# Four gate and up chunks by single token tiles, tile 1's LN2 transposed by DMA, W_down loaded later in halves

## The chip, the cores and the metric

The kernel runs on one core of a Trainium2 chip. The metric is the device time of one launch in microseconds (us), given as the median of the shown runs. The kernel before takes 271.42 us (three runs: 271.40, 271.42 and 271.55).

## The reference

One transformer block over 2048 tokens of width 640 in bf16: a layer norm, a linear attention of 32 heads of 20 with learned feature maps, the residual, a second layer norm and a gated feed-forward net of width 1536.

```python
def _A_ref(x, wqkv, w_phi, wo):
    qkv = (x @ wqkv).reshape(B, S, 3, H, Dh).transpose(2, 0, 3, 1, 4)
    q, k, v = qkv[0], qkv[1], qkv[2]
    pq = jnp.einsum("bhsd,hdf->bhsf", q, w_phi)
    pk = jnp.einsum("bhsd,hdf->bhsf", k, w_phi)
    phi_q = jnp.concatenate([_softmax(pq), _softmax(-pq)], axis=-1)
    phi_k = jnp.concatenate([_softmax(pk), _softmax(-pk)], axis=-1)
    kv = jnp.einsum("bhsf,bhsd->bhfd", phi_k, v)
    z = jnp.einsum("bhsf->bhf", phi_k)
    num = jnp.einsum("bhqf,bhfd->bhqd", phi_q, kv)
    den = jnp.einsum("bhqf,bhf->bhq", phi_q, z)[..., None] + 1e-6
    return (num / den).transpose(0, 2, 1, 3).reshape(B, S, D) @ wo

def _B_ref(x, w_gate, w_up, w_down):
    return (_gelu(x @ w_gate) * (x @ w_up)) @ w_down

h = x + _A_ref(_layernorm(x), A_wqkv, A_w_phi, A_wo)
h2 = h + _B_ref(_layernorm(h), B_w_gate, B_w_up, B_w_down)
```

## The kernel before

The 2048 tokens are 16 tiles of 128, in four blocks of four tiles. The kernel has two phases. The first normalises x (LN1), forms V and the key features of every tile and sums the attention state KV over all tiles. The second, which the change touches, forms the query features (q_mm, q_exp), applies the state to each token tile, projects with Wo, adds the residual, normalises again (LN2) and runs the gated net.

**The steps of a token tile t in the second phase.** attn_a: 40 small matmuls (tile "ab", L586) apply the state; their results are copied from PSUM to SBUF as AB (L653), by ScalarE or, with the argument dve, by VectorE. attn_b and attn_b2: denominators and weights, pr, den and w on GpSimd and the reciprocal rd on VectorE. attn_b3: on VectorE tt (L683) and o (L687), then a DMA on SyncE's queue transposes o into oT. attn_c: the projection with Wo, 10 matmuls into po (L708). attn_d: VectorE adds the residual into x_sb and takes a sum. attn_d2: ScalarE squares, GpSimd works out mean and deviation. attn_e: ScalarE writes the normalised ln (L151), and it is transposed into LN2T, a block's 512 columns wide. Tiles 0 and 1 are treated apart, ahead of the others: their ln comes from VectorE (L156), tile 0's goes through a DMA transpose (L167), tile 1's, by attn_e(1, True, True) at L879, through five TensorE transposes into a PSUM tile "tp" (L164) that VectorE copies out (L165).

**The gated net.** gate_up(b, f, a0, a1) at L759 is one chunk: 128 of the 1536 hidden columns for the tokens a0 to a1 of block b. Five matmuls with W_gate and five with W_up (L768), the token columns moving, give the two halves of a PSUM tile gu; ScalarE writes the gelu g (L771), VectorE the product GT (L774). For block 0 the first round takes 256 tokens (tiles 0 and 1), 12 chunks, the next round the other 256; later blocks take 512. down(b, tl, u, ...) at L776 multiplies one token tile's 12 chunks of GT with W_down (L790), each chunk's GT as the loaded weight, in the order f = 0 to 11, and VectorE adds the residual (L792).

**What sets the order.** Every engine's order is that of the program, which is written out by hand. weave(units, stages) at L811 goes through a list of units (the chunks, then the W_down products); ahead of unit i it runs the stages whose number is at most i. attn_at(t, i, offs) at L885 gives the unit numbers of tile t's eight steps as i plus an offset; a negative offset leaves a step out, as tile 2's attn_a is called ahead of the weave (L882).

**PSUM.** Until the stage split, at unit 12, all of these results share a pool of four tiles, two banks each (gtile, L111, bufs=4 at L80): pq, tp, each of the two tiles of an ab, po, and each gu. A tile is taken again once its last reader is done. After split the banks are handed out singly.

**DMA.** All the DMAs of this phase are issued on SyncE's queue, in program order; an issue that waits holds up those behind it. load_down((f, n)) loads n of the 12 parts of W_down: nine parts at L870, three as a stage at unit 6 (L898).

Of the kernel before, what the change touches and what calls it, by code (L numbers as in the profile page):

```python
# [8 lines left out]
BF16 = mybir.dt.bfloat16  # L9
F32 = mybir.dt.float32  # L10
ALU = mybir.AluOpType
ACTF = mybir.ActivationFunctionType
# [5 lines left out]
def kernel(  # L18
# [12 lines left out]
    nc = tc.nc  # L31
    P = 128
# [7 lines left out]
    NC = D // P  # L40
    NF = FF // P
# [46 lines left out]
    Wg = const.tile([P, NC, FF], BF16, name="Wg")  # L88
    Wu = const.tile([P, NC, FF], BF16, name="Wu")
# [6 lines left out]
    Eq = [const.tile([P, len(g), 2, 512], BF16, name=f"Eq{j}") for j, g in enumerate(QG)]  # L96
# [14 lines left out]
    def gtile(name):  # L111
        return psG.tile([P, 2, 512], F32, name=name, tag="G")
# [46 lines left out]
    def transpose_to(dst, src, on_pe, on_dve=False):  # L159

        if on_pe:
            tp = psG.tile([P, 16, P], BF16, name="tp", tag="G")
            for c in range(NC):
                nc.tensor.transpose(tp[:, c, :], src[:, c * P:(c + 1) * P], ident)  # L164
            (nc.vector.tensor_copy if on_dve else nc.scalar.copy)(dst, tp[:, 0:NC, :])  # L165
        else:
            nc.sync.dma_start_transpose(dst, src)  # L167
# [219 lines left out]
    def q_mm(j, part=(0, 1), kcs=range(NC)):  # L387

        if 0 in part and 0 in kcs:
            pqs[j] = gtile("pq")  # L390
        for i, bc in enumerate(QG[j]):
            if i not in part:
                continue
            b, c = divmod(bc, NC)
            for kc in kcs:
                nc.tensor.matmul(pqs[j][:, i, :], lhsT=Wq2[:, kc, c * P:(c + 1) * P], rhs=LN1T[b][:, kc, :],  # L396
                                 start=(kc == 0), stop=(kc == NC - 1))

    def q_exp(j, signs=(0, 1)):
        for s in signs:  # L400
            nc.scalar.activation(Eq[j][:, :, s, :], pqs[j][:, 0:len(QG[j])], ACTF.Exp, scale=(1.0, -1.0)[s])  # L401
# [135 lines left out]
    q = len(QT)  # L537
# [10 lines left out]
    p2 = ctx.enter_context(tc.tile_pool(name="p2", bufs=1, reuse_waits="tile"))  # L548
    p2r = ctx.enter_context(tc.tile_pool(name="p2r", bufs=1, side="right", reuse_waits="tile"))
    Wd = p2r.tile([P, NF, D], BF16, name="Wd")  # L550
# [6 lines left out]
    def load_down(*fs):  # L557

        for f, n in fs:
            nc.sync.dma_start(Wd[:, f:f + n], wd_v[:, f:f + n])  # L560
# [3 lines left out]
    LN2T, st = {}, {}  # L564
# [6 lines left out]
    def bank(name):  # L571
        return psB[0].tile([P, 512], F32, name=name, tag="B")

    def attn_a_mm(t):

        b = t // 4
        if b not in LN2T:
            LN2T[b] = p2.tile([P, NC, 512], BF16, name="LN2T", bufs=2)
        st[t, "ab"] = gtile("ab"), gtile("ab")
        ab = [x[:, i] for x in st[t, "ab"] for i in range(2)]  # L580
        for s in range(2):
            for c in range(NC):
                i, h, n = SLOT[c]
                h += s * QH
                for r, q in enumerate(QUAD):
                    nc.tensor.matmul(ab[r][:, h * KC:(h + n) * KC], lhsT=eq(t, c, s)[q],  # L586
                                     rhs=KV[s][q, i:i + n, 1 - s:1 - s + KC],
                                     start=(s == c == 0), stop=(s == 1 and c == NC - 1), skip_group_check=True)
        st[t] = ab
# [59 lines left out]
    def attn_a(t, dve=0):  # L649
        attn_a_mm(t)  # L650
        AB, ab = ABs[t % 2], st[t, "ab"]
        for u in ((1, 0) if t in (4,) else (0, 1)):
            (nc.vector.tensor_copy if u >= 2 - dve else nc.scalar.copy)(  # L653
                AB[:, :, u * UH:(u + 1) * UH].rearrange("p s (r h) f -> p r s (h f)", r=2),
                ab[u][:, :, 0:2 * QH * KC].rearrange("p r (s x) -> p r s x", s=2))
        st[t] = AB
# [73 lines left out]
    def attn_ds(t, between=None):  # L730

        st[t] = ln_stats(p2, [x_sb[t // 4][:, t % 4, :]], "2", False, between)[0]
# [17 lines left out]
    def attn_ln(t, on_pe=False):  # L750
        st[t] = (ln_dve if on_pe else ln_act)(p2, "2", *st[t])

    def attn_e(t, on_pe=False, on_dve=False):
        if on_pe is False:
            attn_ln(t)
        ln = st[t]
        transpose_to(LN2T[t // 4][:, :, t % 4 * P:(t % 4 + 1) * P], ln, on_pe, on_dve)

    def gate_up(b, f, a0, a1):  # L759
        if psB:  # L760
            gu = bank("gu"), bank("gu")
        else:
            gu = gtile("gu")
            gu = gu[:, 0], gu[:, 1]
        n = a1 - a0
        for i, W in ((0, Wg), (1, Wu)):
            for c in range(NC):
                nc.tensor.matmul(gu[i][:, 0:n], lhsT=W[:, c, f * P:(f + 1) * P], rhs=LN2T[b][:, c, a0:a1],  # L768
                                 start=(c == 0), stop=(c == NC - 1))
        g = p2.tile([P, 512], BF16, name="g", bufs=3)  # L770
        nc.scalar.activation(g[:, 0:n], gu[0][:, 0:n], ACTF.Gelu_apprx_tanh)  # L771
        if (b, "g", f) not in st:
            st[b, "g", f] = p2.tile([P, 512], BF16, name="GT", bufs=NF + 2)
        nc.vector.tensor_tensor(st[b, "g", f][:, a0:a1], gu[1][:, 0:n], g[:, 0:n], ALU.mult)  # L774
# [28 lines left out]
    def store(n):  # L803

        stores[:] = [(i - n, *x) for i, *x in stores]
        while stores and stores[0][0] <= 0:
            _, dst, src = stores.pop(0)
            nc.sync.dma_start(dst, src)


    def weave(units, stages):  # L811

        stages = sorted(later + stages, key=lambda x: x[0])
        later.clear()
        for i, (fn, *args) in enumerate(units):
            while stages and stages[0][0] <= i:
                _, g, *a = stages.pop(0)
                g(*a)
            store(1)
            fn(*args)  # L820
        later.extend((i - len(units), g, *a) for i, g, *a in stages)

    def gus(b, a0, a1):
        return [(gate_up, b, f, a0, a1) for f in range(NF)]

    def downs(b, tls, pairs={}):

        cut = {tl: DC if u == 0 else D - DC for tl, u in pairs}
        return [(down, b, tl, u, cut.get(tl, HD), pairs.get((tl, u))) for tl in tls for u in range(2)]
# [37 lines left out]
        attn_e(0, None)  # L867

    attn_ds(1, first)
    load_down((0, 9))  # L870
    q_mm(q + 5)
    q_exp(q + 5)
    q_mm(q + 6)
# [2 lines left out]
    q_mm(q + 7)  # L876
    q_exp(q + 7)
    q_mm(q + 8, kcs=(0, 1, 2))
    attn_e(1, True, True)  # L879
    q_mm(q + 8, kcs=(3, 4))  # L880
    q_exp(q + 8)
    attn_a(2, 2)  # L882
    assert q + 9 == len(Eq)

    def attn_at(t, i, offs):  # L885

        fns = (attn_a, attn_b, attn_b2, attn_b3, attn_c, attn_d, attn_d2, attn_e)
        return [(i + o, fn, t) for fn, o in zip(fns, offs) if o >= 0]

    def attn_rest(t, *at):  # L890

        return [(i, fn, t) for fn, i in zip((attn_b, attn_b2, attn_b3, attn_c, attn_d, attn_d2, attn_e), at)]

    SHORT = (0, 2, 3, 4, 10, 10, 11, 13)
    LONG = (0, 1, 2, 5, 5, 6, 7)

    weave(gus(0, 0, 256) + downs(0, (0, 1), {(0, 1): 6}),
          attn_at(2, 0, (-1, 0, 1, 2, 7, 7, 8, 10)) + attn_at(3, 1, (2, 3, 4, 5, 9, 9, 10, 12)) + [(6, load_down, (9, 3))] +  # L898
          attn_at(4, 6, SHORT) + attn_at(5, 9, (0, 2, 5, 6, 11, 11, 12, 14)) + [(12, split)] +
          attn_rest(6, 15, 16, 17, 23, 23, 24, 26) + attn_rest(7, 18, 19, 20, 25, 25, 26, 28))  # L900
    weave(gus(0, 256, 512) + downs(0, (2, 3), {(2, 1): 8, (3, 1): 10}),
          [x for t, i in ((8, 15), (9, 18), (10, 19), (11, 21)) for x in attn_rest(t, *(i + o for o in LONG))])
# [35 lines left out]
```

## Time and profile before

| what | value |
|---|---|
| median of the shown runs | 271.42 us |
| the profiled execution | 272.35 us, with a span of 270.6 us from the first to the last instruction |
| TensorE busy | 266.1 us, 98% of the span |
| VectorE, ScalarE, GpSimd busy | 173.9, 138.6 and 101.2 us |
| granted TensorE clock | 1.00 |

The profile is of one execution. A row of the chain or of a timeline gives start, length in us, engine (PE is TensorE, PEld its weight loads, DVE VectorE, ACT ScalarE, POOL GpSimd, SPq SyncE's DMA queue), the line of the kernel, the operation with output and inputs, and the count; in square brackets stands how long the engine sat idle before it and what ended that. In rows grouped by line the bar is followed by busy time in us and the mean of one in ns. Rows on DMA issues give KB and the time from issue to landing. A matmul's length includes its way through the array, so lengths overlap, and the chain counts only the part that is not overlapped.

### The profile page before, as it was taken

What the parts mean: (1) busy time and instruction counts of PE and PEld (TensorE: products, weight loads), DVE (VectorE), ACT (ScalarE), POOL (GpSimd) and SP (SyncE); (2) the same over time, 40 slices, a digit from 0 to 9 for tenths busy, and PEclk for the clock granted to TensorE, in tenths of its full rate; (3) what the DMA queues carried; (4) which work ended last, traced back from release to release, by engine and by line L of the source; (5) the groups of instructions that cost most, each with busy time, mean ns of one, the idle gap of its engine ahead of it and who ended that gap; (6) DMA issues with size and microseconds to landing.
All of it is one profiled execution on the core that took longest, in us unless ns stands there. A gap on an engine that the chain in (4) does not pass through costs nothing.

```text
span 270.6 us, 7029 instructions
## 1 busy us (share of the span) xinstructions
PE 266.1 (98%) x2857; PEld 172.0 (64%) x2857; DVE 173.9 (64%) x347; ACT 138.6 (51%) x249; POOL 101.2 (37%) x238
## 2 busy tenths in 40 slices
PE   8999999999999999999999999999999999999995
PEld 6777777765455887788755455775555476444574
DVE  5789999996877767876566783568673332333322
ACT  5779997877789675245541356421544300322100
POOL 5448898887002335376211564014661100000000
DMA  6987489213864442432301222203222101000011
GB/s 187 206 199 169 81 210 96 46 37 85 326 201 112 157 101 55 68 78 50 51 27 51 48 50 48 50 3 75 76 46 51 24 24 51 24 0 0 4 48 48
DMA packets 45264, 22.10 MB, mean 82 GB/s; under 512 B 37808, under 2 KB 43184, under 8 KB 45232
## 3 DMA queue, kind: packets, MB, share of 16 engines
q1 hardware_dynamic: 44576, 21.64, 33.5%
q8 instruction: 22, 0.36, 0.6%
q10 hardware_dynamic: 656, 0.03, 0.2%
q14 instruction: 10, 0.08, 0.1%
HBM read 10.18 MB, written 2.62 MB: 47 GB/s over the span
## 4 chain that ended last, share of the span: by engine, by line
PE 96%; DMA 2%; SPq 0%; DVE 0%; issue 0%
PE gu L768 39%; PE pd L790 19%; PE pq L396 8%; PE pk L296 8%; PE po L708 8%; PE pv L296 7%; DMA Wv<-in_A_wqkv_dram 2%; PE kvp L374 2%; PE pv L312 2%; PE ab L619 1%; PE wa L248 1%; PE ab L586 1%; PE tp L164 0%; SPq L193 0%; SPq L190 0%; SPq L189 0%
## 5 line engine op out<-in xcount | busy, mean ns | idle before, releaser
L771 ACT ACTIVATE g<-gu 128x512 bf16<-128x512 f32 (+1 forms) x60 | 30.4, 510 | 74.0 <-PE gu L768 73.2
L774 DVE TENSOR_TENSOR GT<-gu,g 128x512 bf16<-128x512 f32 (+1 forms) x60 | 34.3, 579 | 46.8 <-PE gu L768 38.6
L768 PE MATMUL gu<-LN2T,Wg 128*128 128x512 bf16 (+1 forms) x300 | 61.8, 337 | 0.0
L768 PE MATMUL gu<-LN2T,Wu 128*128 128x512 bf16 (+1 forms) x300 | 61.8, 336 | 0.0
L790 PE MATMUL pd<-Wd,GT 128*128 128x320 bf16 (+4 forms) x396 | 53.9, 295 | 0.0
L790 PEld LDWEIGHTS <-GT 128*128 128x128 bf16 x396 | 37.6, 98 | 14.5 <-DVE GT L774 0.2
L768 PEld LDWEIGHTS <-Wu 128*128 128x128 bf16 x300 | 29.4, 98 | 22.6
L768 PEld LDWEIGHTS <-Wg 128*128 128x128 bf16 x300 | 29.1, 98 | 21.2
L296 PEld LDWEIGHTS <-LN1T 128*128 128x128 bf16 x290 | 28.0, 98 | 10.4
L355 POOL TENSOR_TENSOR E<-E,rs 128x640 bf16<-128x640 bf16 x25 | 31.7, 1295 | 4.4 <-DVE rs L351 2.8
L792 DVE TENSOR_TENSOR y<-pd,x_sb 128x320 bf16<-128x320 f32 (+4 forms) x33 | 15.8, 480 | 24.1 <-PE pd L790 24.1
L708 PE MATMUL po<-Wo,oT 128*128 128x320 bf16 x160 | 24.5, 299 | 0.0
L296 PE MATMUL pk<-Wk,LN1T 128*128 128x320 bf16 x160 | 24.4, 299 | 0.0
L396 PE MATMUL pq<-LN1T,Wq 128*128 128x512 bf16 x100 | 22.9, 379 | 0.0
L347 DVE TENSOR_REDUCE sk<-E 128x64 f32<-128x1280 bf16 x16 | 22.9, 1430 | 0.0
L401 ACT ACTIVATE Eq<-pq 128x1024 bf16<-128x1024 f32 (+1 forms) x26 | 19.9, 831 | 2.8 <-PE pq L396 2.7
L340 ACT ACTIVATE E<-pk 128x640 bf16<-128x640 f32 x28 | 19.1, 769 | 3.0 <-PE pk L296 3.0
L708 PEld LDWEIGHTS <-oT 128*128 128x128 bf16 x160 | 15.6, 98 | 7.3 <-ACT oT L165 0.2
L296 PE MATMUL pv<-Wv,LN1T 128*128 128x320 bf16 x130 | 19.8, 299 | 0.0
L151 ACT ACTIVATE ln<-x_sb,v,rstd 128x640 bf16<-128x640 bf16 x14 | 12.9, 920 | 13.0 <-POOL v L747 12.9
L396 PEld LDWEIGHTS <-Wq 128*128 128x128 bf16 x100 | 9.4, 98 | 10.3
L683 DVE TENSOR_TENSOR tt<-AB,w 128x1280 bf16<-128x1280 f32 x10 | 15.1, 1505 | 0.4 <-POOL w L676 0.3
(120 smaller groups left out, 291.4 us busy)
## 6 DMA issues: line engine op xcount, KB each, us to landing
out_dram<-y SPq DMA_DIRECT2D x15, 160.0 KB, 1.8
x_sb<-in_A_x_dram SPq DMA_DIRECT2D x6, 320.0 KB, 3.3
Wd<-in_B_w_down_dram SPq DMA_DIRECT2D x1, 1440.0 KB, 6.8
Wg<-in_B_w_gate_dram SPq DMA_DIRECT2D x1, 1152.0 KB, 7.3
Wu<-in_B_w_up_dram SPq DMA_DIRECT2D x1, 1152.0 KB, 5.6
Wo<-in_A_wo_dram SPq DMA_DIRECT2D x1, 800.0 KB, 5.0
Wg<-in_B_w_gate_dram SPq DMA_DIRECT2D x1, 768.0 KB
Wu<-in_B_w_up_dram SPq DMA_DIRECT2D x1, 768.0 KB, 9.1
```

The lines of the kernel that those rows point to most:

```text
L296: nc.tensor.matmul(ps[:, u, 0:HD], lhsT=lnT(t, c), rhs=W[:, c, u * HD:(u + 1) * HD], start=(c == 0), stop=(c == NC - 1))
L340: nc.scalar.activation(Ek[t][:, s, :].rearrange("p (u f) -> p u f", u=2), pk[:, :, 0:HD], ACTF.Exp, scale=((lnp[t][2], nrstd[t]) if t in C ...
L347: nc.vector.reduce_sum(sk, Ek[t].rearrange("p s (h f) -> p (s h) f", f=Dh), axis=AX.X)
L355: eng.tensor_tensor(e, e, rs[:, s * H:(s + 1) * H, None].to_broadcast([P, H, Dh]), ALU.mult)
L396: nc.tensor.matmul(pqs[j][:, i, :], lhsT=Wq2[:, kc, c * P:(c + 1) * P], rhs=LN1T[b][:, kc, :], start=(kc == 0), stop=(kc == NC - 1))
L401: nc.scalar.activation(Eq[j][:, :, s, :], pqs[j][:, 0:len(QG[j])], ACTF.Exp, scale=(1.0, -1.0)[s])
L708: nc.tensor.matmul(pos[u], lhsT=st[t][:, c, :], rhs=Wo[:, c, u * HD:(u + 1) * HD], start=(c == 0), stop=(c == NC - 1))
L768: nc.tensor.matmul(gu[i][:, 0:n], lhsT=W[:, c, f * P:(f + 1) * P], rhs=LN2T[b][:, c, a0:a1], start=(c == 0), stop=(c == NC - 1))
L771: nc.scalar.activation(g[:, 0:n], gu[0][:, 0:n], ACTF.Gelu_apprx_tanh)
L774: nc.vector.tensor_tensor(st[b, "g", f][:, a0:a1], gu[1][:, 0:n], g[:, 0:n], ALU.mult)
L790: nc.tensor.matmul(pd[:, 0:f1 - f0], lhsT=st[b, "g", f][:, tl * P:(tl + 1) * P], rhs=Wd[:, f, f0:f1], start=(f == 0), stop=(f == NF - 1), ...
L792: nc.vector.tensor_tensor(y[:, f0:f1], pd[:, 0:f1 - f0], x_sb[b][:, tl, f0:f1], ALU.add)
```

## The change

Four things. gate_up's matmuls are moved into a helper, gu_mm. The first four chunks of block 0's first round are split by token tile: gate_first works on tile 0's 128 columns for four chunks ahead of the weave, gate_second on tile 1's, as units 0 to 3; two chunks share one PSUM tile, one gelu of 512 columns is done for each pair, then two products. Tile 1's LN2 goes through a DMA transpose (attn_e(1, None)). W_down is loaded in two halves of six parts, the first behind a one-column GpSimd copy into its tile that reads the last query features, the second at unit 6. Besides, some steps of tiles 2, 4 and 5 get other unit numbers: tile 2's attn_c, attn_d, attn_d2 and attn_e one unit later; tile 4's attn_a from 6 to 8, attn_b from 8 to 9, attn_b2 from 9 to 10, attn_b3 from 10 to 11; tile 5's attn_a from 9 to 10.

```diff
+    def gu_mm(gu, b, f, a0, a1):
+        for i, W in ((0, Wg), (1, Wu)):
+            for c in range(NC):
+                nc.tensor.matmul(gu[i][:, 0:a1 - a0], lhsT=W[:, c, f * P:(f + 1) * P], rhs=LN2T[b][:, c, a0:a1],
+                                 start=(c == 0), stop=(c == NC - 1))
+
+    def gate_first(f):
+
+        if f % 2 == 0:
+            st[f, "gu"] = gtile("gu")
+        gu = st[f // 2 * 2, "gu"]
+        gu_mm([gu[:, i, f % 2 * 256:f % 2 * 256 + P] for i in range(2)], 0, f, 0, P)
+
+    def gate_second(f):
+
+        f0 = f // 2 * 2
+        gu = st[f0, "gu"]
+        gu_mm([gu[:, i, f % 2 * 256 + P:f % 2 * 256 + 256] for i in range(2)], 0, f, P, 2 * P)
+        if f == f0:
+            return
+        g = p2.tile([P, 512], BF16, name="g", bufs=3)
+        nc.scalar.activation(g, gu[:, 0], ACTF.Gelu_apprx_tanh)
+        for i in range(2):
+            h = slice(i * 256, i * 256 + 256)
+            st[0, "g", f0 + i] = p2.tile([P, 512], BF16, name="GT", bufs=NF + 2)
+            nc.vector.tensor_tensor(st[0, "g", f0 + i][:, 0:256], gu[:, 1, h], g[:, h], ALU.mult)
...
     attn_ds(1, first)
-    load_down((0, 9))
     q_mm(q + 5)
...
     q_mm(q + 8, kcs=(0, 1, 2))
-    attn_e(1, True, True)
+    attn_e(1, None)
     q_mm(q + 8, kcs=(3, 4))
     q_exp(q + 8)
+    nc.gpsimd.tensor_copy(Wd[:, 0, 0:1], Eq[q + 8][:, 0, 1, 0:1])
+    load_down((0, 6))
     attn_a(2, 2)
+    for f in range(4):
+        gate_first(f)
...
-    weave(gus(0, 0, 256) + downs(0, (0, 1), {(0, 1): 6}),
-          attn_at(2, 0, (-1, 0, 1, 2, 7, 7, 8, 10)) + attn_at(3, 1, (2, 3, 4, 5, 9, 9, 10, 12)) + [(6, load_down, (9, 3))] +
-          attn_at(4, 6, SHORT) + attn_at(5, 9, (0, 2, 5, 6, 11, 11, 12, 14)) + [(12, split)] +
+    weave([(gate_second, f) for f in range(4)] + gus(0, 0, 256)[4:] + downs(0, (0, 1), {(0, 1): 6}),
+          attn_at(2, 0, (-1, 0, 1, 2, 8, 8, 9, 11)) + attn_at(3, 1, (2, 3, 4, 5, 9, 9, 10, 12)) + [(6, load_down, (6, 6))] +
+          attn_at(4, 6, (2, 3, 4, 5, 10, 10, 11, 13)) + attn_at(5, 9, (1, 2, 5, 6, 11, 11, 12, 14)) + [(12, split)] +
```

SHORT, tile 4's offsets before, is (0, 2, 3, 4, 10, 10, 11, 13).

More of the change, by code (lines that the diff above doesn't have):

```diff
@@ L765, in gate_up @@
         n = a1 - a0
[L766 to L769, printed above, removed]
+        gu_mm(gu, b, f, a0, a1)
         g = p2.tile([P, 512], BF16, name="g", bufs=3)
```

## The prediction

> **What bounds the kernel now.** I read the page first, for its span and the chain that ended last; then the waits of the weight loads, since a TensorE stall shows in front of a weight load here; then that chain in order of time from 66 to 112 us; and last the timelines of VectorE and ScalarE over the same stretch.
>
> ```profile
> span 270.6 us, 7029 instructions
> ...
> PE 96%; DMA 2%; SPq 0%; DVE 0%; issue 0%
> ```
>
> TensorE is the chain for 96% of the span. Behind the first weights nothing else ends last. Of the waits between 60 us and the end, the one that matters below is the last in the list:
>
> ```profile
> PEld L790 <- DVE GT L774: 0.2, 1, 0.2
> ```
>
> W_down's first product once waited for a gated chunk, 0.2 us, on a load that runs ahead. So TensorE is fed without a gap, but at that place only just. What a part of the change costs is therefore what it adds to TensorE's own work, plus every wait that it opens; nothing downstream gives such time back. The chain in order of time (start, length, work):
>
> ```profile
> 78.42 0.28 PE tp L164 x5
> ...
> 85.27 0.30 PE tp L164 x5
> 85.58 0.43 PE pq L396 x2
> 86.01 0.40 PE ab L586 x40
> 86.41 3.38 PE gu L768 x30
> 89.79 0.40 PE ab L586 x39
> 90.19 3.38 PE gu L768 x30
> ...
> 95.17 1.36 PE po L708 x10
> 96.53 2.18 PE gu L768 x20
> ...
> 103.86 2.46 PE pd L790 x18
> ```
>
> The reader sees tile 1's five transposes at 85.27, tile 2's state products (ab) right behind, the chunks gu0 to gu11 of 1.09 us each (20 matmuls in 2.18), 0.11 more for the first one behind an ab (3.38 less 3 x 1.09), an output projection of 1.36, and W_down from 103.86 at 0.137 a matmul (2.46 for 18).
>
> **TensorE's own work.** Removed: the five transposes, **-0.30** (85.27). Their copy on VectorE held nobody up, as ab started on time. Added: four chunks of 10 matmuls over 256 columns become 80 over 128. The nearest row is a transpose: 128 columns and a weight load of its own each, 0.28 for five, 0.056 each; the other row of five gives 0.060. From below, half of a 256-column matmul is 0.0545 and the cost is nothing; from above, were each paced by its weight load (98 ns, the second row below), 80 x 0.098 = 7.84 against 4 x 1.09 = 4.36, +3.48. I take 0.056, the like operation without a wait in front of it: 4.48, **+0.12**.
>
> ```profile
> L790 PE MATMUL pd<-Wd,GT 128*128 128x320 bf16 (+4 forms) x396 | 53.9, 295 | 0.0
> L790 PEld LDWEIGHTS <-GT 128*128 128x128 bf16 x396 | 37.6, 98 | 14.5 <-DVE GT L774 0.2
> ```
>
> **Tile 1's transpose as a DMA.** LN1's source is there by 85.27, when TensorE uses it. SyncE has nothing else to issue then, because the W_down load that stood there now comes behind.
>
> ```profile
> Wd<-in_B_w_down_dram SPq DMA_DIRECT2D x1, 1440.0 KB, 6.8
> ...
> oT<-o SPq DMA_TRANSPOSE x15, 2.4
> LN2T<-ln SPq DMA_TRANSPOSE x15, 2.6
> ```
>
> 85.3 + 2.6 = 87.9. ab now runs from 85.71 to 86.11 (0.30 earlier), the four tile-0 chunks until 86.11 + 0.11 + 4 x 0.56 = 88.46, and only then is tile 1 wanted: 0.6 to spare, cost nothing. Without that cover, the four narrow chunks, the wait would be 1.8. The first half of W_down is wanted at 104; with 6.8 for the larger load it may be issued as late as 97, so its wait for the small GpSimd copy costs nothing. Behind it on SyncE stands only tile 2's oT transpose, which comes at about 93 (worked out below); behind the copy on GpSimd stands attn_b(2), which waits for VectorE's copies of ab(2) at that time anyway. The second half follows oT of tile 3, at 96.9 by the queue below, whose issue takes 1.34:
>
> ```profile
> L167 SPq DMA_TRANSPOSE oT<-o x1: 1336/1336/1336, 96.5 to 96.5; - x1
> ```
>
> So it goes out at 98.2, and even with 6.8 it lands at 105.0, near 104.9, where matmul f=6 wants it, and what that could cost lies inside the larger wait found below.
>
> **VectorE's queue moves.** Engines take their work in program order. Now the first gated product comes only behind the second gate_second, and behind it the whole of tile 2. The starts in this row give each instruction's pace:
>
> ```profile
> 89.20 0.34 DVE L672 RECIPROCAL rd<-den 128x32 f32<-128x32 f32 x1
> 89.46 0.36 DVE L774 TENSOR_TENSOR GT<-gu,g 128x256 bf16<-128x256 f32 x1
> 90.14 1.49 DVE L683 TENSOR_TENSOR tt<-AB,w 128x1280 bf16<-128x1280 f32 x1 [0.32 <-POOL w L676]
> 91.67 0.49 DVE L687 TENSOR_TENSOR o<-tt 128x640 bf16<-128x640 bf16 x1
> 92.08 1.28 DVE L774 TENSOR_TENSOR GT<-gu,g 128x256 bf16<-128x256 f32 x3
> ...
> 96.29 0.42 DVE L774 TENSOR_TENSOR GT<-gu,g 128x256 bf16<-128x256 f32 x1
> 96.63 0.82 DVE L726 SCALAR_TENSOR_TENSOR x_sb<-po,x_sb 128x640 bf16<-128x640 f32 x1
> ...
> 104.39 0.75 DVE L774 TENSOR_TENSOR GT<-gu,g 128x256 bf16<-128x256 f32 x2
> ```
>
> A product (GT) holds the queue 0.34 (96.29 to 96.63) and is done after 0.42; rd 0.26; tt 1.53; o 0.41; from rd to tt, through GpSimd's w, 0.94. ScalarE's rows:
>
> ```profile
> 93.61 0.38 ACT L771 ACTIVATE g<-gu 128x256 bf16<-128x256 f32 x1 [0.71 <-DVE rd L672]
> ...
> 99.24 1.39 ACT L653 COPY AB<-ab 128x704 f32<-128x704 f32 x2
> 100.52 0.40 ACT L771 ACTIVATE g<-gu 128x256 bf16<-128x256 f32 x1
> ```
>
> gelu starts 0.04 after its chunk (90.19 + 3.38 = 93.57, then 93.61). The two copies of AB hold ScalarE 1.28 (99.24 to 100.52); they start 0.13 behind ab, which ended at 96.53 + 2.18 + 0.40 = 99.11. I give a product the same 0.04 behind its gelu. The wide gelu takes 0.60:
>
> ```profile
> L771 ACT ACTIVATE g<-gu 128x512 bf16<-128x512 f32 x36 | 21.5, 596 | 63.2 <-PE gu L768 63.2
> ```
>
> The second gate_second ends at 88.46 + 1.12 = 89.58; gelu 89.62 to 90.22; GT0 at 90.26, GT1 90.60, tt(2) 90.94, o(2) 92.47, GT2 92.88, GT3 93.22, GT4 93.56, rd(3) 93.90, GT5 94.16, tt(3) 93.90 + 0.94 = 94.84, o(3) 96.37, GT6 96.78 and done at 97.20. GT7 follows at 97.12, the residual of tile 2 at 97.46. oT(2) lands at 92.47 + 0.49 + 2.4 = 95.4. TensorE meanwhile: gate_second 2 until 90.14, ab(3) 90.54, gate_second 3 91.21, gu4 to gu7 95.57 (gu4's PSUM tile comes free with GT1 at 91.02), po(2) 96.93.
>
> **Wait one, a PSUM tile.** Next comes attn_a(4), moved from unit 6 to unit 8. It needs two of the four G tiles. One holds po(2) until the residual at 97.46, one gu6 until GT6, one gu7 until GT7: a single tile is free. The second comes at 97.20. A load follows its releaser by 0.05:
>
> ```profile
> 105.19 0.79 PEld L790 LDWEIGHTS <-GT 128*128 128x128 bf16 x7 [0.15 <-DVE GT L774]
> ```
>
> (the two products of 104.39 end at 105.14). With 0.07 more, as a cold ab's chain piece begins, it starts at 97.32 instead of 96.93: **+0.39**. The price goes from 0 (VectorE 0.4 earlier) to 0.9 (the tile of the residual, 97.46 + 0.82, is the one that is given). Then ab(4) 97.72, gu8 98.92, gu9 100.01, po(3) 101.37 (its oT landed at 99.3), ab(5) 101.77, gu10 102.97, gu11 104.06, against 103.86 before.
>
> **Wait two, W_down's last chunk.** Tile 4's tt and o moved from unit 10 to unit 11: before, they ran ahead of GT10 and GT11 (104.39); now they stand between the two. ScalarE is late as well, with ab(5) one unit later: its copies run 101.90 to 103.18, gelu10 to 103.56, GT10 at 103.60, tt(4) 103.94, o(4) 105.47, GT11 105.88, done 106.30, load 106.35. Matmul f=11 would start at 104.06 + 11 x 0.137 = 105.56 and end at 105.70; it ends at about 106.35 + 0.30 = 106.65 (295 ns for one alone, the first of the two rows on L790): **+0.95**. This hangs little on the first wait, since all of it follows gu10. From below 0.7 (no copies ahead of gelu10, 0.17, and a queue as much quicker as the rounding of its terms allows); from above 1.7, if tile 4's w is late for tt(4): it stands behind GpSimd's work on tile 2's residual, which starts at 97.46, 0.8 later than now.
>
> **Sum.** -0.30 + 0.12 + 0.39 + 0.95 = **+1.16** on a span of 270.6. The profiled execution took 272.35, 1.75 beside its span; the shown runs have a median of 271.42, 0.93 below it. I put the sum on the median: **272.6**.
>
> **Rivals.** *Neither wait (271.2).* It needs one thing: that VectorE does a chunk's product ahead of the tt and o written before it, so that GT6 follows gelu6 at 95.4 and GT11 gelu11 at 105. Then -0.30 + 0.12 = -0.18, not slower. For it speaks only that the order is read from the code and not from a trace of the changed kernel; against it the row at 92.08, where three products stand in a heap behind tt and o. It decides once GT6 is done before 96.8 and GT11 before 105.5.
>
> *The W_down wait alone (272.2).* VectorE gains 0.4 between 90.3 and 97.2, or a buffer is free: 1.16 - 0.39 = +0.77. For it: my times are sums of a dozen terms. Against: nothing in that queue waits but tt(3).
>
> *The PSUM wait alone (271.6).* 1.16 - 0.95 = +0.21, if tt(4) starts ahead of GT10. The order of units speaks against it.
>
> *Narrow matmuls paced by their weight loads (275.5).* +3.48 - 0.30 + 0.95; TensorE then comes late enough at attn_a(4) for the first wait to vanish. For it: 98 ns a load against 54 of streaming. Against it: five transposes with five loads in 0.28. The Trainium skill ("TensorE: Matmul & The Clock Gate", Back-to-back issue gap) says that a stream of load and matmul pairs runs at about 81 ns a matmul of 128 columns; by that page this would be an estimated +2.1 for the 80 matmuls and some 274.2 in all. The trace's 56 to 60 ns for such pairs stands against the page, over five in a row only.
>
> **Chances.** Forecast with both waits 0.62; W_down alone 0.10; PSUM alone 0.09; neither 0.14; weight loads 0.05. The forecast's own bounds, -0.30 + 0.12 + (0 to 0.9) + (0.7 to 1.7), give 271.9 to 273.8; both upper ends at once are unlikely, so 271.9 to 273.4. The range takes in the single waits and leaves out the neither and the weight loads (0.19): 271.5 to 273.4. A measurement of this kernel can tell about 0.2%, 0.54 us, from no change. Faster by more than that needs more than the 0.30 that is removed: 0.04, kept out of neither's share for what the trace does not show. Within: the rest of neither (0.10) and PSUM alone (0.09), less a little that such a wait comes out larger: 0.17. Slower 0.79.
>
> **What would show it.** Right: no tp at 85, 80 matmuls of 128 columns at 0.056; a wait of 0.3 to 0.5 in front of the ab behind po(2), ended by GT on VectorE; one of 0.9 at the twelfth W_down matmul, ended by GT L774, with tt and o between the last two products; no wait for LN2T or Wd. Wrong: narrow matmuls 0.08 or more apart; a wait for a DMA; VectorE out of the written order; or any wait before 97 us.

## The result and the profile after

The changed kernel takes 273.98 us (median of five runs, 273.75 to 274.15), the kernel before 271.42 on the same chip: 2.56 more, a ratio of 1.0093 with a 95% interval of 1.0078 to 1.0108. The direction was foretold, the size was not: 272.6 was predicted, and the range ended at 273.4. The profiled execution took 273.75.

From the page of the changed kernel, the chain's shares by engine:

```profile
PE 93%; DMA 3%; DVE 1%; ACT 1%; SPq 0%; issue 0%; ACTq 0%
```

TensorE, 96% of the chain before, has lost three points, and a DMA, VectorE and ScalarE now stand in it. TensorE's waits in front of a matmul from 60 us to the end (us in total, times, longest), where before there was none:

```profile
PE po L708 <- DMA oT<-o: 0.8, 1, 0.8
PE pd L814 <- DVE GT L798: 0.8, 1, 0.8
PE gu L762 <- ACT AB L653: 0.2, 1, 0.2
```

Three waits, where two were predicted. The chain in order of time shows what each costs:

```profile
65.97 0.87 PE kvp L374 x96
...
85.39 4.01 PE gu L762 x70
89.41 0.49 PE ab L586 x39
...
89.92 0.75 ACT AB L653
90.68 0.04 issue
90.72 4.53 PE gu L762 x40
95.25 0.94 PE po L708 x7
96.19 3.86 DMA oT<-o
...
100.10 1.53 PE po L708 x10
...
104.21 1.49 DVE tt L683
...
105.72 0.49 DVE o L687
106.22 0.34 DVE GT L798
...
106.61 1.11 PE pd L814 x7
...
108.55 4.17 PE pd L814 x30
```

The whole projection of tile 3 (100.10) hangs on its transposed oT, which took 3.86 from issue to landing. The kernel before has, for the first and the last of these pieces:

```profile
66.68 0.87 PE kvp L374 x96
...
107.14 4.17 PE pd L790 x30
```

The way from TensorE's last sum of the attention state (kvp) to the second half of W_down's first burst is the measure used from here on, **the stretch**: 107.14 - 66.68 = 40.46 before, 108.55 - 65.97 = 42.58 after, **+2.12**. It leaves out the start, where the first weights take a different time in each execution: this profile comes to kvp 0.71 earlier than that of before, which is why the spans, 270.6 and 272.0, differ by 1.4 only. The medians differ by 2.56. Behind the stretch both profiles take 163.5 to the end, so the other 0.44 lie in the start, or in executions other than the profiled ones; they were not traced.

The +2.12 are made up of TensorE's own work, -0.18 as predicted, and three waits. The first, in front of the fifth chunk, is read from starts:

```profile
90.03 0.44 PE L762 MATMUL gu<-LN2T,Wu 128*128 128x128 bf16 x5
90.72 0.71 PE L762 MATMUL gu<-LN2T,Wg 128*128 128x256 bf16 x5 [0.25 <-ACT AB L653]
```

Five at 0.056 from 90.03 would have let the next start at 90.31: 0.41 (the 0.25 in brackets is less, since an instruction's length includes its way through the array). The wait for oT is worth 0.80 of idle time and 0.17 by which ten po matmuls behind a stall take longer (1.53 against 1.36), 0.97. What is left, 2.12 + 0.18 - 0.41 - 0.97 = 0.92, is the wait of the twelfth W_down matmul for GT11. The rows bear this out: 0.77 of idle time, and 0.15 by which the seven matmuls behind it take longer (1.11 against 7 x 0.137).

### The profile page after: what moved, and what is told of

Read it like the earlier page. It is cut to its first block, busy times and chain, and to the rows that moved or that the text cites. A ratio compares the mean times of both kernels' runs of the same rounds, so it can differ in the third digit from the quotient of the medians.

```text
span 272.0 us, 7096 instructions
## 1 busy us (share of the span) xinstructions
PE 265.9 (98%) x2892; PEld 171.8 (63%) x2892; DVE 173.6 (64%) x346; ACT 138.5 (51%) x247; POOL 100.3 (37%) x239
## 4 chain that ended last, share of the span: by engine, by line
PE 93%; DMA 3%; DVE 1%; ACT 1%; SPq 0%; issue 0%; ACTq 0%
PE gu L762 37%; PE pd L814 19%; PE pq L396 8%; PE pk L296 8%; PE po L708 8%; PE pv L296 7%; PE kvp L374 2%; DMA Wv<-in_A_wqkv_dram 2%; PE pv L312 2%; DMA oT<-o 1%; PE ab L619 1%; PE wa L248 1%; PE ab L586 1%; ACT AB L653 1%; DVE tt L683 1%
## 5 line engine op out<-in xcount | busy, mean ns | idle before, releaser
L795 ACT ACTIVATE g<-gu 128x512 bf16<-128x512 f32 (+1 forms) x56 | 29.0, 519 | 71.3 <-PE gu L762 71.3
L798 DVE TENSOR_TENSOR GT<-gu,g 128x512 bf16<-128x512 f32 (+1 forms) x56 | 32.8, 592 | 47.7 <-PE gu L762 39.2
L762 PE MATMUL gu<-LN2T,Wg 128*128 128x512 bf16 (+2 forms) x320 | 62.5, 326 | 0.2 <-ACT AB L653 0.2
L762 PE MATMUL gu<-LN2T,Wu 128*128 128x512 bf16 (+2 forms) x320 | 62.4, 326 | 0.0
L762 PEld LDWEIGHTS <-Wu 128*128 128x128 bf16 x320 | 30.0, 98 | 22.4
L762 PEld LDWEIGHTS <-Wg 128*128 128x128 bf16 x320 | 29.7, 98 | 21.3 <-issue 0.4
L340 ACT ACTIVATE E<-pk 128x640 bf16<-128x640 f32 x28 | 18.5, 730 | 3.0 <-PE pk L296 3.0
```

Source lines behind the costliest of these rows:

```text
L340: nc.scalar.activation(Ek[t][:, s, :].rearrange("p (u f) -> p u f", u=2), pk[:, :, 0:HD], ACTF.Exp, scale=((lnp[t][2], nrstd[t]) if t in C ...
L762: nc.tensor.matmul(gu[i][:, 0:a1 - a0], lhsT=W[:, c, f * P:(f + 1) * P], rhs=LN2T[b][:, c, a0:a1], start=(c == 0), stop=(c == NC - 1))
```

## The experiments

Each run is compared with runs of the kernel before on the same chip, whose medians were 271.58 (e1 to e4), 271.86 (e5 to e8), 271.79 (e9 to e11) and 271.89 (e12).

e3's stretch is left out, since TensorE waits inside the burst at which it ends. The landing is the time from the issue of tile 3's oT to its landing.

| run | over the kernel before, us | ratio, 95% interval | stretch | oT(3) landing |
|---|---|---|---|---|
| the change | 2.56 | 1.0078 to 1.0108 | 42.58 | 3.86 |
| e1 | 2.71 | 1.0090 to 1.0119 | 42.95 | 4.23 |
| e2 | 2.06 | 1.0064 to 1.0088 | 42.32 | 3.93 |
| e3 | 2.42 | 1.0074 to 1.0100 | | 3.85 |
| e4 | 0.70 | 1.0018 to 1.0050 | 41.09 | 2.6 |
| e5 | 3.07 | 1.0093 to 1.0125 | 43.23 | 4.50 |
| e6 | 0.63 | 1.0010 to 1.0033 | 40.85 | 4.03 |
| e7 | 1.86 | 1.0046 to 1.0088 | 42.48 | 2.4 |
| e8 | 1.43 | 1.0044 to 1.0068 | 41.91 | 2.9 |
| e9 | 4.10 | 1.0119 to 1.0159 | 42.76 | 2.6 |
| e10 | 0.30 | 0.9995 to 1.0014 | 40.51 | 3.6 |
| e11 | 3.76 | 1.0130 to 1.0169 | 42.53 | 2.8 |
| e12 | 3.18 | 1.0097 to 1.0134 | 41.61 | 2.6 |

### Is it W_down's second half? (e1)

```diff
-attn_at(3, 1, (2, 3, 4, 5, 9, 9, 10, 12)) + [(6, load_down, (6, 6))] +
+attn_at(3, 1, (2, 3, 4, 5, 9, 9, 10, 12)) +
...
-rhs=Wd[:, f, f0:f1]
+rhs=Wd[:, f % 6, f0:f1]
```

> The changed kernel without the second load of W_down: the products of chunks 6 to 11 use parts 0 to 5 again, so the matmuls are as many and as long. My theory: oT of tile 3 took 3.9 us to land in the changed kernel (2.4 for tile 2's) because 960 KB of W_down were issued right behind it, and po(3) waited for it. Without that load oT(3) lands in 2.4 to 2.6, the wait of 0.8 to 1.0 in front of po(3) is gone, and the time falls from 273.98 to about 273.0. The wait at the twelfth W_down matmul stays at 0.9 or a little more. Rival: the transpose is late by itself, whatever stands behind it: 3.9 again and 274.0.

Measured: 274.29, +2.71 over the kernel before. The load that stands behind oT(3) is gone, and oT(3) takes 4.23, TensorE's wait for it 1.2. The second half of W_down does not delay the transpose; this theory fell.

### The wait for GT11 (e2, e3)

e2 moves tile 4's tt and o back to unit 10, ahead of GT10:

```diff
-attn_at(4, 6, (2, 3, 4, 5, 10, 10, 11, 13))
+attn_at(4, 6, (2, 2.5, 3, 4, 10, 10, 11, 13))
```

> Tile 4's attn_b3 (tt and o on VectorE) goes back from unit 11 to unit 10, ahead of GT10, its attn_b and attn_b2 a little earlier so that w is there. Simple theory of the prediction: the wait at W_down's twelfth matmul was VectorE's order alone; it goes, -0.9, about 273.05. Rival: ScalarE's order holds the last chunk as well. Behind gelu10 stand there the normalised ln of tile 2 (0.93) and the squares of tile 3 (0.95), and only then gelu11; then GT11 comes only 0.2 earlier and 0.7 of the wait stays, about 273.75, with gelu11 as what VectorE waited for.

Measured: 273.64; the stretch is 0.26 shorter. Two of TensorE's waits in e2, the third being unchanged:

```profile
PE po L708 <- DMA oT<-o: 0.9, 1, 0.9
PE pd L814 <- DVE GT L798: 0.3, 1, 0.3
```

The wait for GT11 falls from 0.8 to 0.3, and 0.1 of that goes to a longer one for oT: tt and o between the last two products do hold up W_down, but with them out of the way ScalarE is next, whose ln and sq stand ahead of the last gelu in e2's chain. e3 moves those two later as well:

```diff
-attn_at(2, 0, (-1, 0, 1, 2, 8, 8, 9, 11)) + attn_at(3, 1, (2, 3, 4, 5, 9, 9, 10, 12))
+attn_at(2, 0, (-1, 0, 1, 2, 8, 8, 9, 12)) + attn_at(3, 1, (2, 3, 4, 5, 9, 9, 11, 12))
-attn_at(4, 6, (2, 3, 4, 5, 10, 10, 11, 13))
+attn_at(4, 6, (2, 2.5, 3, 4, 10, 10, 11, 13))
```

> As the run with tile 4's attn_b3 at unit 10, and in addition ScalarE's ln of tile 2 and squares of tile 3 stand behind gelu11 (units 12). If VectorE's and ScalarE's orders together make the wait at W_down's twelfth matmul, it is gone now: -0.9, about 273.05, in the trace no wait on a GT at W_down. Rival: something else holds GT11 (the chunk itself, a PSUM tile): 0.5 or more of the wait stays, 273.5 or more. The wait of po(3) for oT(3) should stand in both, 0.8 to 1.0.

Measured: 274.0, no better than e2. The wait for GT11 is gone, and one of 0.4 behind ScalarE's copies of the state products of tiles 6 and 7 takes its place: what was taken from in front of the gelu now stands in front of those copies.

### The unit numbers alone (e4)

```diff
-attn_at(2, 0, (-1, 0, 1, 2, 8, 8, 9, 11))
+attn_at(2, 0, (-1, 0, 1, 2, 7, 7, 8, 10))
-attn_at(4, 6, (2, 3, 4, 5, 10, 10, 11, 13)) + attn_at(5, 9, (1, 2, 5, 6, 11, 11, 12, 14))
+attn_at(4, 6, SHORT) + attn_at(5, 9, (0, 2, 5, 6, 11, 11, 12, 14))
```

> The change with tile 2's, 4's and 5's steps at the unit numbers of the kernel before: the split chunks, the DMA transpose and the two halves stay. My theory by the queues: the retimed steps cost most. po(2) comes one unit earlier and waits some 0.2 for oT(2), ab(4) 0.4 for a PSUM tile, po(3) 0.3 for oT(3), and the wait at W_down is almost gone since tt and o of tile 4 run ahead of GT10: about -1.4, 272.6. Rival: the split and the loads make the loss whatever the units, then it stays within 0.4 of 274.0.

Measured: 272.28, +0.70; the stretch is +0.63 over the kernel before. Of the 2.12, 1.49 are gone with the old unit numbers (42.58 - 41.09): the wait for GT11, and that for oT(3), which lands 2.6 after its issue. In front of two weight loads 0.3 is left each, one for oT(2), since po(2) comes one unit earlier again, and one behind the second half of W_down, which lands at 104.23. Two things differ at once here, the order of the steps and the time of the 16 KB packets of which the next part speaks (one at 94.39 in place of 97.42), so this run alone doesn't say why the transpose was late.

### What delays the transpose (e5, e6, e9, e11, e12)

The list of DMA queues has, beside the kernel's own transfers, 22 packets of 16 KB named "instruction", spread over the span, and 10 of 8 KB on a second queue of that name; the 0.36 MB of the first queue for TensorE's 2892 matmuls and 2892 loads are 62 bytes an instruction. The theory: the 16 KB packets are blocks of TensorE's program, fetched as it advances, and one that falls among the packets of a transpose delays it. The 1 us around the block near oT(3), in the kernel before and in the changed kernel (forty slices of busy tenths, then the packets by queue), and below it the packets of a later window:

```profile
DMA  0090000000000000000000000009000000000000
...
q8 instruction: 1, 0.02, 5.6%
...
DMA packets 672, 0.16 MB, mean 117 GB/s; under 512 B 672, under 2 KB 672, under 8 KB 672
```

```profile
DMA  9679999999999999999999190000900000000000
...
q1 hardware_dynamic: 495, 0.13, 222.6%
q8 instruction: 1, 0.02, 6.8%
...
DMA packets 175, 0.04 MB, mean 31 GB/s; under 512 B 169, under 2 KB 175, under 8 KB 175
```

Before (the first fence, 96.4 to 97.4), the block starts at 96.45 and has the engines to itself (5.6% of 16 engines in 1 us, so 0.90). The last line is of 97.4 to 98.8: a transpose of this size is 672 packets under 512 bytes, and all of them ran there. For this oT(3) the trace has no landing, but its packets had ended 2.3 after the issue at 96.5, and po(3) did not wait. After (97.4 to 98.4), the block starts at 97.42 among 495 packets of the transpose, issued at 96.2. The last line is of 98.2 to 99.6: 169 of the 672, a quarter, are left over and run only there. The 8 KB packet near by (97.1 before, 96.9 after) comes ahead of the transpose's packets in both kernels, so it doesn't make the difference.

All fourteen traces say the same. From 70 us on they have 394 transposes of this size with a landing. In 273 of these no packet of either instruction queue runs in the first 2.3 us behind the issue: each of them lands after 2.36 to 2.71. In 53 a 16 KB block runs among the packets (1.17 to 2.05 behind the issue): they take 2.77 to 4.50, half of them 3.85 or more.

To move the block is the test of the cause. Ten fewer warm-up matmuls at the start should move each block 20 instructions later in the computation. e5 does so in the changed kernel, e6 in the one before:

```diff
-    warm(*[512] * 2, *[P] * 28)
+    warm(*[512] * 2, *[256] * 10, *[P] * 8)
```

> The changed kernel with 10 fewer matmuls at the very start, in the stretch that waits for the first weights: 10 of 256 and 8 of 128 columns in place of 28 of 128, the same columns in all. My new theory for the late oT of tile 3: a 16 KB block on the DMA queue named instruction moved from 97.4 to 98.5 us in the changed kernel, while the transpose's packets ran, and in the run without the second half from 97.6 to 99.1; in the kernel before it moved from 96.45 to 97.3, ahead of the packets. The page counts 22 such blocks of 16 KB for TensorE's 5784 instructions (64 bytes each), so 20 instructions fewer put the block some 1.1 us later, behind the packets. Then oT(3) lands in 2.4 to 2.6, the wait in front of po(3) is gone and the time falls by 0.8 to 1.0, to about 273.05. Rival: the transpose is slow by its place in the queue or by what else runs then: 3.9 again, within 0.3 of 274.0.

> The kernel before with the same 10 matmuls fewer at the start and nothing else. By the instruction-block theory the block of 96.45 moves to about 97.55, into the packets of tile 3's oT, which then lands 3.5 to 4.2 us after its issue instead of about 2.0 to 2.5; po(3) waits for it 0.2 to 0.6, and the time rises to about 271.8 to 272.1. Rival: the count of instructions plays no part, oT lands as before and the time stays at 271.4 to 271.6.

e5 measured 274.93: the block did not move against the computation (98.26, with everything 0.86 later from the start on), oT(3) took 4.50, and the gain expected was missed. Why these 20 instructions moved nothing here is open. e6 measured 272.49, and there the block moved from 96.45 to 97.29. The window of 97.2 to 98.2, the waits and the chain of e6:

```profile
q1 hardware_dynamic: 493, 0.13, 214.1%
q8 instruction: 1, 0.02, 10.1%
```

```profile
PEld L708 <- DMA oT<-o: 0.5, 1, 0.5
```

```profile
96.43 4.03 DMA oT<-o
...
100.50 1.53 PE po L708 x10
```

The kernel before, with none of the change in it, has now the same late transpose (4.03; without the block its packets had ended 2.3 after the issue) and the same wait on the chain; its stretch is 0.39 longer. Of the 0.63, 0.24 lie outside the stretch. The block makes the lateness without the change.

e9 and e12 shift the blocks the other way in the changed kernel, by 34 and 18 instructions; e11 joins e9 and e2.

```diff
-    warm(*[512] * 2, *[P] * 28)
+    warm(512, *[P] * 28, *[8] * 10)
...
-    warm(*[P] * 4)
+    warm(*[8] * 12)
```

> The changed kernel with 17 more tiny matmuls in the two warm-up bursts at the start (the first burst has one matmul of 512 columns and 28 of 128 and then 10 of 8 columns, the second 12 of 8 columns in place of 4 of 128; their products are read by nobody), so 34 more instructions lie ahead of everything else on TensorE and each 16 KB instruction block is fetched 34 instructions earlier in the computation, some 1.5 to 2.5 us. Instruction-block theory: the block whose packets lay at 97.42 in the changed kernel comes between 94.9 and 96.2, ahead of tile 3's oT packets (97.35 to 98.3); oT(3) lands 2.4 to 2.8 us after its issue in place of 3.86, the first po matmul of tile 3 waits 0 to 0.3 in place of 0.97, and from TensorE's last kvp burst to the second half of the first pd burst it is 41.6 to 41.9 us in place of 42.58; 0.7 to 1.0 less than the changed kernel, 1.5 to 1.9 over the one before. Rival, that the transpose is late because it leaves later than in the kernel before, beside W_down's second half: oT(3) stays at 3.5 to 4.3, the stretch at 42.4 to 42.8, and the time within 0.3 of the changed kernel's. The longer bursts may start the first weights' matmuls up to 0.5 later, which the stretch leaves out.

> The edits of e2 (tile 4's last normalising step from unit 11 to unit 10) and of e9 (34 more instructions at the start) together. If the two waits, for oT(3) and for GT11, are separate and add up, the stretch from the last kvp burst to the second half of the first pd burst is 42.58 less 0.97 less 0.26 to 0.5, so 41.0 to 41.4, which leaves the PSUM wait of 0.4 at the fifth gate and up chunk and up to 0.5 of the GT11 wait over the 40.46 of the kernel before; the time is 0.6 to 1.0 over the kernel before. If one wait hides in the other (TensorE, no longer held at po(3), runs ahead and waits longer for GT11), the wait for GT11 grows to 0.8 or more and the stretch stays above 41.6.

e9 measured 275.89 and e11 275.55, both worse than the change. In both the block had gone too far: from tile 3's transpose into tile 2's. The chain of e9:

```profile
94.26 3.91 DMA oT<-o
...
98.22 1.53 PE po L708 x10
```

This is oT(2), issued at 94.26 and landing after 3.91, with the block at 96.08 among its packets, while oT(3) landed after 2.6. The lateness moved with the block; the time did not fall, and the start took 1.99 longer (kvp at 67.96). The expected shift was off: 34 instructions were worth 3.3 us (97.42 to 96.08, less the 1.99) and not 1.5 to 2.5. The second half of e11's question, whether the waits add up, got no clean answer, because oT(2) was late in place of oT(3); between e9 and e11, the b3 edit was worth 0.23.

e12 keeps only the first of the two lines of e9:

```diff
-    warm(*[512] * 2, *[P] * 28)
+    warm(512, *[P] * 28, *[8] * 10)
```

> The changed kernel with 9 more matmuls in the first warm-up burst (10 of 8 columns in place of one of 512; read by nobody), 18 more instructions on TensorE ahead of everything. In e9, with 34 more, the 16 KB block went from 97.42 to 96.08, which is 94.1 once its later start (the kvp burst at 67.96 in place of 65.97) is taken off: past tile 3's oT packets and into tile 2's, whose transpose took 3.91 while tile 3's was on time. With 18 it should fall between the two, at 95.4 to 96.5 in the changed kernel's clock (the block of the kernel before lay at 96.45 and took 0.89). Block theory: both transposes land 2.4 to 2.8 after their issue, no po matmul waits more than 0.3, and the stretch from TensorE's last kvp burst to the second half of the first pd burst is 41.4 to 41.8 in place of 42.58; the wait for GT11 stays or grows by up to 0.4, since TensorE comes to it earlier (then 41.8 to 42.0). Rival, that some transpose of this stretch is late in the changed kernel wherever the block lies, because two or more transfers share the queue: one of the two takes 3.5 or more, and the stretch stays at 42.4 to 42.8.

The block came at 95.62, between the two transposes, which landed after 2.4 and 2.6. The chain of e12:

```profile
65.93 0.87 PE kvp L374 x96
...
90.68 4.53 PE gu L762 x40
95.21 1.36 PE po L708 x10
...
99.26 1.36 PE po L708 x10
...
107.54 4.17 PE pd L814 x30
```

No DMA stands in the stretch, which is 41.61, 0.97 shorter than that of the change, inside what was expected. The rest of the sum is -0.18 + 0.41 + 0.92 = +1.15 over the kernel before. All the same e12 measured 275.07, not less than the change. In its profile a later transpose is late, tile 7's, issued at 122.64, with a block at 124.43 among the last of its packets, and TensorE's weight load waits for it:

```profile
PEld L708 <- DMA oT<-o: 1.3, 1, 1.3
```

Tile 7's projection starts at 126.63, where the changed kernel has it at 126.61: the 0.97 were given back there. That the median lies still higher (the six runs spread from 273.93 to 275.69) was not traced. From the first to the last instruction, the medians of e12 and of the kernel before beside it are 272.85 and 270.15, 2.70 apart; so 0.48 of the 3.18 lie outside that span.

### Narrow chunks or wide (e8)

The chunks are 256 columns wide again, the old unit numbers stand, and tile 1's DMA transpose and the halves of W_down are kept:

```diff
-    for f in range(4):
-        gate_first(f)
...
-    weave([(gate_second, f) for f in range(4)] + gus(0, 0, 256)[4:] + downs(0, (0, 1), {(0, 1): 6}),
+    weave(gus(0, 0, 256) + downs(0, (0, 1), {(0, 1): 6}),
```

> The change without the split: the first four chunks take 256 columns again, unit numbers as before; tile 1's DMA transpose and the two halves of W_down stay. The prediction put the wait of the first chunk for tile 1 at 1.8 without the cover of the narrow chunks. With -0.30 for the removed transposes, and everything behind it late alike: about +1.5, 272.9 to 273.1, and in the trace a wait of TensorE for LN2T of 1.6 to 1.9 at gu0. Rival: the transposed tile lands sooner than its 2.6 and the wait is under 1: 272.2 or less.

Measured: 273.29; TensorE's only wait is the one that the narrow chunks cover.

```profile
PE gu L762 <- DMA LN2T<-ln: 1.7, 1, 1.7
```

The prediction put the price of that cover at 1.8.

### Putting it right (e7, e10)

e7 moves tiles 2 and 3 one unit ahead, as far as the narrow chunks run ahead of the units, and puts tiles 4 and 5 back:

```diff
-attn_at(2, 0, (-1, 0, 1, 2, 8, 8, 9, 11)) + attn_at(3, 1, (2, 3, 4, 5, 9, 9, 10, 12))
+attn_at(2, 0, (-1, 0, 0.5, 1, 7, 7, 8, 10)) + attn_at(3, 1, (1, 2, 3, 4, 9, 9, 10, 12))
-attn_at(4, 6, (2, 3, 4, 5, 10, 10, 11, 13)) + attn_at(5, 9, (1, 2, 5, 6, 11, 11, 12, 14))
+attn_at(4, 6, SHORT) + attn_at(5, 9, (0, 2, 5, 6, 11, 11, 12, 14))
```

> The change with the old unit numbers, and besides tile 2's rd, tt and o on VectorE ahead of the first two products, and tile 3's attn_a to attn_b3 one unit earlier. By the queues: tile 2's and 3's oT are issued about 1 us earlier, so no wait for a transpose at po(2) and po(3); ab(3) and its copies come before gate_second 2, so gu4 finds its PSUM tile; what is left is up to 0.2 at gu6 and 0.1 at W_down. Sum -0.05 to +0.2 against the kernel before: 271.4 to 271.8. Rival: if the split chunks and the DMA route cost something that does not hang on these steps, it stays at the 272.3 of the old unit numbers.

Measured: 273.72. TensorE waited for no transpose (oT(2) and oT(3) landed after 2.8 and 2.4), and the three waits were gone from their places; 0.4 was left in front of a chunk, with no releaser shown, and a new wait stood at the first W_down matmul:

```profile
PE pd L814 <- DVE GT L798: 1.3, 1, 1.3
```

The first pd takes bank 0 of the single banks that split hands out. In e7 the last chunk before split sits in that very tile, so the first product waits until GT11 has read it. e10 lets a tiny matmul take that turn:

```diff
+    def turn():
+        nc.tensor.matmul(gtile("turn")[:, 0, 0:8], lhsT=ones[:, 0:P], rhs=ones[:, 0:8], start=True, stop=True)
...
-[(12, split)]
+[(11, turn), (12, split)]
```

> The kernel of e7 (tiles 2 and 3 ahead by one unit, tiles 4 and 5 at the old unit numbers) with one matmul of 8 columns into a PSUM tile of its own ahead of the twelfth gate and up chunk, read by nobody: it takes the turn of slot 0, so that chunk 11 sits in slot 3 and the first W_down matmul, whose bank is always bank 0 of the new pool, no longer needs GT11. Bank theory of e7's wait: the wait of 1.3 at the first W_down matmul goes, and GT11 is needed only by that burst's twelfth matmul, 11 x 0.146 = 1.6 later; the stretch from the last kvp burst to the second half of the first pd burst is 41.0 to 41.4 in place of 42.48, so 0.5 to 1.0 over the kernel before, 0.9 to 1.4 under the changed kernel (272.4 to 273.0 us). Rival, that the first W_down matmul waits for VectorE being behind with its queue and not for a bank: the same wait of 1.0 or more appears at the first or at the twelfth matmul, and the stretch stays at 42.2 or more.

Measured: 272.09, a ratio of 1.0004 (0.9995 to 1.0014): no difference from the kernel before can be told. The chain of e10:

```profile
66.16 0.87 PE kvp L374 x96
...
91.03 0.76 DVE GT L787 x2
...
91.83 1.25 PE gu L765 x10
...
102.28 1.11 PE gu L765 x10
103.39 2.46 PE pd L817 x18
...
106.67 4.17 PE pd L817 x30
```

W_down runs without a gap, and the wait of e7 was the bank. oT(3) was late here as well, 3.6 after its issue at 95.4, with an 8 KB packet of the second instruction queue at 97.28 among its packets; with the issue nearly 1 us earlier than in the change this cost nothing, since po(3) begins at 99.7 only. The stretch is 40.51, better than the 41.0 to 41.4 expected. What separates it from 40.46 - 0.18 = 40.28 is about the size of the one wait left, that of the sixth chunk (91.83) for a PSUM tile that the products of 91.03 release. No version beat the kernel before: with every wait out of the way, narrow chunks and DMA transpose have 0.18 to give.

## Why the prediction was wrong

**The step that failed: "its oT landed at 99.3".** The landing of oT(3) was taken as 2.4 after its issue, the median of the 15 transposes before. It took 3.86, and po(3) waited: 0.97, the whole difference between the predicted +1.16 and the stretch's +2.12. A median was taken as the time of each. In the very trace that it is from, the oT issued at 112.3 took 4.2, with a 16 KB block at 114.08 among its packets; TensorE did not wait for it, so no list of waits showed it:

```profile
L167 SPq DMA_TRANSPOSE oT<-o x1: 1217/1217/1217, 112.3 to 112.3; - x1
...
DMA to landing us min/median/max: 4.2/4.2/4.2
```

The 2.4 holds on the condition that no instruction block falls among the packets; e6 shows the transpose of tile 3 late in the kernel before when one does, e9 and e12 that the lateness follows the block. That a block fell just there in the changed kernel is chance, as far as the runs show. "A wait for a DMA" was named as what would show the prediction wrong; none of its rivals had it, and the range had no room for it.

**TensorE's own work, right.** The 70 matmuls of 128 columns at 85.39 took 4.01, with 0.11 for the cold start 0.0557 each; predicted was 0.056. The rival of weight loads fell. By the Trainium skill ("TensorE: Matmul & The Clock Gate", Back-to-back issue gap) they would have come about 81 ns apart; the trace does not agree.

**Tile 1's transpose and its cover, right.** What the prediction calls LN1's source is the normalised ln of tile 1; its transpose was issued at 84.4 and landed after 2.6. No wait for LN2T in the changed kernel, 1.7 without the cover (e8), 1.8 in the prediction. No wait for either half of W_down.

**Wait one, right in size by luck, wrong in place.** 0.41 measured, 0.39 predicted, but it stood in front of the fifth chunk and not of ab(4). "gu4's PSUM tile comes free with GT1" named the wrong tile: it got one of ab(3)'s two, which ScalarE's copy of 89.92 released. TensorE being late from there, ab(4) found its tiles free. Without that wait the predicted one would have come, an estimated 0.37: GT6 ended at 96.45, and TensorE, which began ab(4) at 96.61, would have been there at 96.20. The wait that did come was also one ahead of 97 us, another thing that was to show the prediction wrong.

**Wait two, right.** The row of tt and o between the last two products stands in the chain as described, 0.92 against 0.95. tt started at 104.21, which is 104.92 by the clock of the profile before; predicted was 103.94, and the 0.98 between are the wait for oT. e2 shows that this order is the cause of the greater part: 0.5 of the 0.8 idle go with it. The rest went in e3, with ScalarE's ln and sq ahead of the last gelu, which the prediction had not named.

**The sum on the median.** Even the stretch's +2.12 would have given 273.5, above the range; the 0.44 between that and 273.98 stay open. Runs of e12 alone spread over 1.8, so a start-up that varies with the instruction stream may be part of it, but no run shows this.

## What to carry to other kernels

A median is not yet a price: look at the longest of the row too, ask what else shared the resource then, and whether the change moves the one against the other; here edits that only added or removed TensorE instructions at the very start moved the instruction blocks behind them in e6, e9 and e12, though not in e5. When steps are re-timed by hand, follow for each buffer which tile of the pool it will get and which reader releases it, since two of the waits met here (the fifth chunk, and bank 0 in e7) were of that kind. And compare two profiles over a stretch that leaves out the start, or a start-up that differs by 0.7 hides a third of the effect.

## What the hardware showed

A 16 KB packet on the "instruction" queue, which takes 0.90 us where it is alone (the kernel before), makes a transpose of a 128x640 tile late, mostly by 1 to 2 us, when it falls among its packets: for tile 3's oT 3.85 to 4.50 in place of 2.4 to 2.6, in six of these kernels (the change, e1, e2, e3, e5 and e6), for tile 2's in e9 and e11 (3.91 and 4.09), for one that nobody waited for in the kernel before (4.2). The transpose's data are 0.16 MB in 672 packets; in the changed kernel a quarter of them are late. An 8 KB packet of the second instruction queue among the packets goes with smaller delays in most cases (e11's oT(3), 2.8), once with a larger one (e10's, 3.6); no run moved it on purpose. Which of TensorE's instructions sets off a fetch was worked out from shifts only: 34 instructions more moved it 3.3 us, 18 more 1.8, 20 fewer 0.84 in e6 and not at all in e5.
